# Linear attention with a Mish MLP on one core: the k v product of items 8 and 9 and the copy before the last addition moved, items 4 to 7 worked in pairs, the first sixteen slots in another order

## The chip, the core and the metric

One core of a Trainium2 chip runs the whole program. Its five engines work from queues of their own: TensorE (PE, the matmuls; PEld is its loading of weights), VectorE (DVE), ScalarE (ACT), GpSimd (POOL) and SyncE (SP, which here only issues transfers). An instruction runs when those ahead of it in its queue are done and its semaphores are set. The metric is the time of one execution on the device, in microseconds; the median of several runs is compared.

## The reference

```python
q_s = softmax(q, axis=-1)                 # over the 64 of a head
k_s = softmax(k, axis=2)                  # over the 576 positions
kv  = einsum('bhsd,bhse->bhde', k_s, v)   # 64 x 64 for each head
x   = einsum('bhsd,bhde->bhse', q_s, kv)  # then heads side by side: 4608 x 512
h   = x @ w_in                            # 512 -> 2048
g   = h * tanh(log1p(exp(h)))             # Mish
out = g @ w_out                           # 2048 -> 512
```

q, k and v have 8 batches of 8 heads, 576 positions of 64. All is float32.

## The kernel before

An *item* is a pair of heads of one batch, so there are 32, four to a batch (`HP = 4`); items i and i+1 share what the code calls a pair. An item passes through: loading; q less its maximum, exp, the sum over each head, its reciprocal and the product (`a_qmax`, `a_qsub`, `a_exp`, `a_qsum`, `a_qinv`, `a_qmul`); k less its maximum over positions and exp; the product k^T v with a column of ones beside v, which brings the sum of exp k; its division by that sum into the tile `kvt`, block by block for two items (`a_kvs2`); transposes of q; and x = q kv for both items (`a_xp`, `a_x2`). x is split into a high and a low part, as are the weights, and three products of the parts give one of full precision.

The MLP works on chunks of 512 tokens: nine chunks, and 2048 hidden units in 16 blocks of 128 make 9 × 16 = 144 *slots*. Slot n has an input product H (`h_part`, `ph`, line 543; four parts of three matmuls of 128x512), Mish on ACT (`y`), a high part gh and a low part gl on DVE (`g_hi`, `g_lo`), and, three slots later (`LAG = 3`), an output product O (`out_part`, `po`, line 596; four parts of three matmuls) that adds to the chunk's four PSUM banks a to d. After a chunk's last slot the four banks are evicted (`evac`, `ob`, line 601) and stored. H takes the banks g and h in turn.

The first sixteen slots run while the first batch and the second are prepared and the weights are converted. Their order is written out in the string `FIRST`, one token for a step, for all engines alike: L, LK, LQ, V, R issue loads on SP's queue (k, transposed k, q, v, a weight unit); MQ, SQ, EQ, Q, QZ, QM work on q; MK, KD, KT, EK, B, KS on k; KP, S are k^T v and kvt; T, TC, XT, XP, Z, ZL, ZT, ST the way to x; RA to RS convert weight units (16 of w_in and 16 of w_out) with bit operations on ACT, DVE and POOL; H, Y, G, GL, O the slots (H4f is the first part of slot 1 in bank f). D or A at the end of a step's name means DVE or ACT in place of the usual engine: SD subtracts and QD multiplies q on DVE (SQ, QM: POOL), KD subtracts k's maximum on DVE, RD, RS and RO, RL are the same weight step on DVE or POOL, GA is the high part on ACT (G: DVE). `FILL` adds dummy matmuls ahead of a step so that PE does not sit idle; the SP queue is in the order of the L, R and V tokens. `STAGED` names the buffer into which each weight unit is loaded.

Items 4 to 7, the second batch, keep k as rows of 128 positions: `a_kmax` transposes the maximum with PE (line 303), `a_ksub` subtracts on DVE over 128x640 (line 337), and `a_kvi` multiplies in matmuls of 128 rows by 64 columns, ten for an item (line 447; the profile counts each twice, 40 for a pair). Items from 8 on (`COLS = 8`) come in pairs: the tile of k holds both items, one on partitions 0 to 63 and the other on 64 to 127, and 36 matmuls of 64 rows by 64 columns (line 487; 72 in the profile) serve both.

After `FIRST` the function `group(n)` issues four slots at a time, and with them the steps of later items. At u = 2 of an odd group it calls `a_pair`, which makes x of one pair and k^T v of the next. The group at i = 8 (slots 16 to 19, with slots 13 to 16 as outputs) is an exception:

```python
if u == 2 and front:      # pairs from 8 on
    g_mish(m)
    a_pair(pair)
...
if 0 <= o < NSLOT:
    out_mm(o)
...                       # evictions, g_hi, g_lo, a_kmx
if u == 2 and not front:  # the pair of items 8 and 9
    a_pair(pair)
```

The products of a pair, `pt`, lie in the banks g and h, which the slots use in turn, and `kvt` is read out of them on DVE. The program's end: the outputs of the last three slots are done bank by bank, banks a to c are evicted with ACT and stored, and the last bank's sum of the earlier slots is copied to `base` by ACT (line 711) after that; the rest of its sum is formed in two fresh half banks, added to `base` by DVE (line 717) and stored by ACT's queue and SP's.

Of the kernel before, what the change touches and what calls it, by code (L numbers as in the profile page):

```python
# [15 lines left out]
P = 128  # L16
# [27 lines left out]

FILL = dict(
    KT1=21, KP0=6, T0=2, KT3=4, H0=2)

STAGED = (
    "xb0 xb3 wo4 xb1 wo5 wo6 wo7 xb2 wo8 wo9 wo10 wo11 wo12 wo13 wo14 raw wo6 wo7 xb2 wo8 wo10 wo9 wo11 wo12 wo13 "
    "raw wo14 wo12 wo13 raw wo14 raw")  # L50
# [3 lines left out]
def attn_mish_mlp(ctx: ExitStack, tc: tile.TileContext, q, k, v, k2, v2, wu, qs, kt, out):  # L54
# [4 lines left out]
    HP, D = 4, k.shape[-1]  # L59
# [122 lines left out]
    ap.tile([P, 76], F32, tag="gap0", name="gap0")  # L182
# [8 lines left out]
    v_last = lp.tile([P, 2 * VC], F32, tag="v3", name="v3")  # L191
    v_two = v_last[:, 0:2 * NR * (D + 2)].rearrange("p (h c f) -> p h c f", h=2, f=D + 2)

    def k_load(i):
        if i >= NITEM:
            return
        r = at[i] = at.get(i, {})
        if i >= COLS:
            t = r["k"] = xp.tile([P, NR, 2, D], F32, tag="raw", name=f"k{i}")
            nc.sync.dma_start(t, k2[(i - COLS) // 2])  # L200
            return
        if i == 6:
            t = pools["ke"]
        else:
            pool, tag = (ap, "ke") if i in (4, 7) else (lp, "k3")
            t = pool.tile([P, NC + 1, 2, D], F32, tag=tag, name=f"k{i}")
        r["k"] = t
        nc.sync.dma_start(t, k[i])
# [23 lines left out]
    def v_load(i):  # L232
        if i >= NITEM:
            return
        if i >= COLS:
            nc.sync.dma_start(v_two, v2[(i - COLS) // 2])
            return
        if i < HP:
            at.setdefault(i, {})["v"] = vt[i] if i < HP - 1 else v_last[:, 0:VC]
            nc.sync.dma_start(at[i]["v"], v[i])  # L240
            return
        for j in range(2):
            at.setdefault(i + j, {})["v"] = v_last[:, j * VC:(j + 1) * VC]
        nc.sync.dma_start(v_last.rearrange("p (i f) -> p i f", i=2), v[i:i + 2].rearrange("i p f -> p i f"))

    def a_kmx(i):
# [4 lines left out]
        nc.vector.tensor_reduce(mxd, r["kt"], axis=AX.X, op=ALU.max)  # L251
# [47 lines left out]
    def a_kmax(i, b):  # L299
        r = at[i]  # L300
        pb = bank(b, f"pb{i}")
        fill(f"B{i}", pb)
        nc.tensor.transpose(pb[:, 0:P], r["mxd"].to_broadcast([P, P]), ident)
        r["mb"] = pb[:, 0:P]
# [9 lines left out]
    def a_ktsub(i, eng=nc.vector):  # L314
        r = at[i]
        eng.tensor_scalar(r["kt"], r["kt"], r["mxd"], None, ALU.subtract)
# [15 lines left out]
    def a_ksub(i):  # L332
        if i >= NITEM:
            return
        r = at[i]
        mb = r["mb"].rearrange("p (h d) -> p h d", h=2)
        nc.vector.tensor_tensor(r["k"], r["k"], mb.unsqueeze(1).to_broadcast([P, NC + 1, 2, D]), ALU.subtract)
# [16 lines left out]
    def a_exp(i, which="kq"):  # L354
        if i >= NITEM:
            return
        r = at[i]
        for nm in which:
            if i < COLS:
                e = r[nm]  # L360
            else:
                e = ap.tile([P, NB, 32], F32, tag="qe", name=f"qe{i}")
            nc.scalar.activation(e, r[nm], AF.Exp)  # L363
            r[nm + "e"] = e
# [85 lines left out]
    def a_kvp(e, b):  # L450
        pkv = bank(b, f"pkv{e}")
        fill(f"KP{e}", pkv)
        for i in range(2):
            a_kvi(pkv[:, i * (D + 2):(i + 1) * (D + 2)], e + i)
        at[e]["pkv"] = pkv[:, 0:2 * (D + 2)].rearrange("p (i f) -> p i f", i=2)

    def a_kvs2(e):
        pkv = at[e]["pkv"]
        rs = ap.tile([P, 2], F32, tag="rs0", name=f"rs{e}")
        if e < COLS:  # L460
            nc.vector.tensor_scalar_add(rs, pkv[:, :, D], 1e-9)
            nc.vector.reciprocal(rs, rs)
            nc.vector.tensor_tensor(kvt, pkv[:, :, 0:D], rs.unsqueeze(2).to_broadcast([P, 2, D]), ALU.mult)
            return
# [6 lines left out]
    def a_pair(e):  # L471
# [10 lines left out]
        if f < NITEM:  # L482
            for c in range(NR):
                for j in range(2):
                    for i in range(2):
                        a = slice(i * D, (i + 1) * D)
                        nc.tensor.matmul(pkv[i][j * D:(j + 1) * D], at[f]["k"][a, c, j], v_two[a, j, c],  # L487
                                         start=c == 0, stop=c == NR - 1)
            at[f]["pkv"] = pkv
# [60 lines left out]
    def open_pools():  # L550
# [4 lines left out]
        op = ctx.enter_context(tc.tile_pool(name="op", bufs=1))  # L555
        pools["ke"] = op.tile([P, NC + 1, 2, D], F32, tag="ke", name="ke_odd")
# [22 lines left out]
    def out_mm(n):  # L579
# [4 lines left out]
        for t in range(NC):  # L584
# [26 lines left out]
    def group(n):  # L611
# [4 lines left out]
        front = pair is not None and pair >= COLS  # L616
        for u in range(G):
# [3 lines left out]
            if u == 2 and front:  # L621
                g_mish(m)
                a_pair(pair)
# [13 lines left out]
            if 0 <= o < NSLOT:  # L637
                out_mm(o)
            if m < NSLOT and not (u == 2 and front):
# [36 lines left out]
        a_exp(i + 1, "q")  # L676
# [6 lines left out]
        KD=a_ktsub, KE=lambda i: a_ktsub(i, pool), KT=a_ktt,  # L683
        EK=lambda i: a_exp(i, "k") if i >= HP else a_ktexp(i), EQ=lambda i: a_exp(i, "q"),
# [9 lines left out]
    with tc.manual_schedule(engines={ET.Activation, ET.PE, ET.DVE, ET.Pool, ET.SP}):  # L694
# [9 lines left out]
        end = range(NSLOT - LAG, NSLOT)  # L704
        for t in range(NC - 1):
# [4 lines left out]
        base = sp.tile([P, DM], F32, tag="wc", name="base")  # L710
        nc.scalar.copy(base, po[t])
# [63 lines left out]
```

## Time and profile before

| | |
|---|---|
| median of 3 runs | 862.34 us (861.81 to 862.42) |
| the profiled execution | 863.62 us, span 861.8 us |
| mean granted clock of PE | 0.998 |
| PE, busy | 848.1 us, 98% |
| DVE, ACT, POOL, busy | 434.3, 320.8, 127.4 us |
| PE idle ahead of H, largest releaser | 2.6 us, DVE kvt |

The profiled execution lies 1.3 us above the median. The span runs from the first to the last instruction. A row of the timeline gives the start, the time from the first start to the last end, engine, line, operation and tile, and in square brackets how long the engine sat idle before it and what released it. Consecutive matmuls overlap, so two starts tell more than one duration.

### The profile page before, as it was taken

To read this page: it belongs to the slowest core of one execution; us is meant where nothing else is said; L and a number is where in the kernel's file an instruction comes from. 1 tells how busy PE (TensorE), PEld (TensorE's weight loads), DVE (VectorE), ACT (ScalarE), POOL (GpSimd) and SP (SyncE) were. 2 spreads that over 40 slices of the span, in tenths; PEclk is the share of its full clock that TensorE was granted. 3 is DMA by queue.
4 is the path that set the end of the run, shared out by engine and by line. 5 is a ranking of instruction groups with operands and counts; after the bars stand their busy time and mean duration, and the time that the engine had idled before them with its cause. 6 is when DMAs were issued, how large, how long until landed. Compare 5 with 4: busy or idle time off the path is not lost.

```text
span 861.8 us, 12412 instructions
## 1 busy us (share of the span) xinstructions
PE 848.1 (98%) x4879; PEld 691.6 (80%) x4879; DVE 434.3 (50%) x1113; ACT 320.8 (37%) x496; POOL 127.4 (15%) x111
## 2 busy tenths in 40 slices
PE   8999998999999999999999999999999999999998
PEld 7777777888888888888888888888888888888886
DVE  7989765554655456554645464546543222222221
ACT  5997644424342524333342434243523111111111
POOL 6895310111111111011111001111110000000000
PEclk9999999999999999999999999999999999999999
DMA  9983224212211122212221222122000020001001
GB/s 352 396 313 117 75 100 136 71 41 73 83 46 64 29 86 77 87 29 84 80 74 41 74 80 70 42 60 76 18 15 1 15 74 13 1 0 49 1 1 49
DMA packets 33211, 66.65 MB, mean 77 GB/s; under 512 B 11520, under 2 KB 11776, under 8 KB 33152
## 3 DMA queue, kind: packets, MB, share of 16 engines
q1 hardware_dynamic: 32752, 65.33, 23.0%
q8 instruction: 38, 0.62, 0.3%
q10 hardware_dynamic: 400, 0.52, 0.2%
q14 instruction: 21, 0.17, 0.1%
HBM read 55.35 MB, written 10.49 MB: 76 GB/s over the span
## 4 chain that ended last, share of the span: by engine, by line
PE 88%; DMA 4%; ACT 3%; DVE 3%; issue 1%; SPq 0%; DVEq 0%; ACTq 0%
PE po L596 43%; PE ph L543 42%; PE px L429 2%; DMA q<-in_q_dram 1%; PE pt L487 1%; DMA kt<-in_kt_dram 1%; DMA raw_in<-in_w_dram 1%; ACT wa L132 1%; DVE wa L148 1%; DVE wc_out L154 1%; ACT ph L561 1%; DVE gl L113 0%; DMA raw_out<-in_w_dram 0%; ACT wih L167 0%; DVE mxd L251 0%
## 5 line engine op out<-in xcount | busy, mean ns | idle before, releaser
L543 PE MATMUL ph<-xs,wih 128*128 128x512 f32 x1152 | 357.6, 392 | 5.5 <-DVE kvt L469 2.6
L596 PE MATMUL po<-wo,gh 128*128 128x512 f32 x1146 | 355.1, 391 | 0.0
L543 PEld LDWEIGHTS ph<-xs,wih 128*128 128x128 f32 x1152 | 215.6, 188 | 53.8 <-issue 3.5
L596 PEld LDWEIGHTS po<-wo,gh 128*128 128x128 f32 x1146 | 214.3, 188 | 45.4 <-issue 0.8
L565 ACT ACTIVATE y<-ph 128x512 f32<-128x512 f32 x128 | 76.5, 597 | 422.6 <-PE ph L543 355.8
L543 PE MATMUL ph<-xs,wil 128*128 128x512 f32 x576 | 225.1, 391 | 0.0
L596 PE MATMUL po<-wo,gl 128*128 128x512 f32 x573 | 223.1, 389 | 0.0
L570 DVE CAST gh<-y 128x512 fp32r<-128x512 f32 x128 | 55.3, 432 | 271.1 <-ACT y L565 271.1
L543 PEld LDWEIGHTS ph<-xs,wil 128*128 128x128 f32 x576 | 108.4, 188 | 22.7
L596 PEld LDWEIGHTS po<-wo,gl 128*128 128x128 f32 x573 | 107.6, 188 | 22.6
L113 DVE TENSOR_TENSOR gl<-y,gh 128x512 fp32r<-128x512 f32 x128 | 89.4, 698 | 11.9
L386 POOL TENSOR_TENSOR qe<-qe,qs 128x576 f32<-128x576 f32 x24 | 27.8, 1160 | 304.0 <-DVE qs L382 304.0
L113 POOL TENSOR_TENSOR q<-q,qm 128x576 f32<-128x576 f32 (+1 forms) x31 | 36.6, 1182 | 191.3 <-DVE qm L270 174.3
L565 ACT ACT_TABLE_LOAD x23 | 29.5, 1283 | 49.0 <-PE ph L543 48.9
L523 DVE TENSOR_TENSOR xs<-px,xs 128x512 fp32r<-128x512 f32 x32 | 20.7, 686 | 49.6 <-ACT xs L520 49.6
L372 DVE TENSOR_REDUCE qs<-qe 128x18 f32<-128x576 f32 x24 | 18.0, 752 | 25.8 <-ACT qe L363 25.8
L352 ACT ACT_TABLE_LOAD x23 | 29.5, 1283 | 2.4 <-DVE k L113 2.0
L279 DVE TENSOR_REDUCE qm<-q 128x18 f32<-128x576 f32 (+1 forms) x32 | 24.3, 762 | 4.9 <-DMA q<-in_q_dram 4.8
L251 DVE TENSOR_REDUCE mxd<-kt 128x1 f32<-128x576 f32 x32 | 23.8, 745 | 2.4 <-DMA kt<-in_kt_dram 2.4
L601 DVE COPY ob<-po 128x512 f32<-128x512 f32 x16 | 11.1, 691 | 26.9 <-PE po L596 26.8
L113 POOL TENSOR_TENSOR wo<-wc_out,wo 128x512 fp32r<-128x512 f32 x15 | 19.4, 1295 | 23.3 <-ACT wo L167 23.2
L363 ACT ACT_TABLE_LOAD x16 | 20.5, 1283 | 4.3 <-DMA q<-in_q_dram 4.0
(112 smaller groups left out, 563.3 us busy)
## 6 DMA issues: line engine op xcount, KB each, us to landing
kt<-in_kt_dram SPq DMA_DIRECT2D x32, 288.0 KB, 2.8
raw_in<-in_w_dram SPq DMA_DIRECT2D x16, 512.0 KB, 8.6
raw_out<-in_w_dram SPq DMA_DIRECT2D x16, 512.0 KB, 6.3
out_dram<-ob SPq DMA_DIRECT2D x32, 256.0 KB, 2.2
v<-in_v_dram SPq DMA_DIRECT2D x12, 594.0 KB, 5.3
q<-in_qs_dram SPq DMA_DIRECT2D x24, 288.0 KB, 2.8
k<-in_k_dram SPq DMA_DIRECT2D x12, 576.0 KB, 4.1
q<-in_q_dram SPq DMA_DIRECT2D x8, 320.0 KB, 6.1
```

The lines of the kernel that those rows point to most:

```text
L113: eng.tensor_tensor(out, a, b, ALU.subtract)
L251: nc.vector.tensor_reduce(mxd, r["kt"], axis=AX.X, op=ALU.max)
L279: nc.vector.tensor_reduce(qm, qt, axis=AX.X, op=ALU.max)
L352: nc.scalar.activation(k2, k2, AF.Exp)
L363: nc.scalar.activation(e, r[nm], AF.Exp)
L372: nc.vector.tensor_reduce(z, q2, axis=AX.X, op=ALU.add)
L386: eng.tensor_tensor(q2, q2, z.unsqueeze(2).to_broadcast(list(q2.shape)), ALU.mult)
L523: nc.vector.tensor_tensor(xs[i][:, 1], src, xs[i][:, 0].bitcast(F32), ALU.subtract)
L543: nc.tensor.matmul(gs[n], wi[a][:, t, fs], x[:, z], start=t == 0 and i == 0, stop=t == HP - 1 and i == 2)
L565: nc.scalar.activation(y, gs[n], AF.Mish)
L570: copy(hi, gs[n])
L596: nc.tensor.matmul(dst, g[a][:, t * P:(t + 1) * P], wo[f][:, z, e], start=first and i == 0, stop=last and i == 2)
```

## The change

1. *The group at i = 8.* `a_pair`, which here makes k^T v of items 8 and 9, is called in the same place as for the later ones, after `g_mish`, and slot 15's output is cut in two: banks a and b ahead of the pair's products, c and d behind them.
2. *The end.* The copy to `base` is issued before the last three slots' outputs and the three evictions.
3. *Items 4 to 7* are loaded, subtracted, exponentiated and multiplied in pairs, as items from 8 on: `in_k_dram` is gone, the layouts of `in_k2_dram` and of `in_v2_dram` begin at item 4, one k load of 576 KB stands in place of two of 320, `a_kmax` puts both maxima in a bank with two matmuls of 64 columns, and `a_kv2` is the 36 matmuls as a function.
4. *The first sixteen slots.* `FIRST`, `FILL` and `STAGED` are new. Three of the first four subtractions of k's maximum run on ACT (token KA, with the maximum negated by its reduction, `negate=i < HP`), one on DVE. Three products of q run on DVE (QD), none did; no subtraction of q does (SD), one did. Of the high parts of the first 16 slots 7 run on ACT, 6 did.

```diff
 FIRST = (
-    "LQ1 LQ0 LK1 LK0 LK2 LQ2 V1 MQ1 LQ3 V0 MQ0 SQ1 LK3 R0 V2 MK1 SQ0 EQ1 V3 MK0 R1 LQ4 KD1 R2 KD0 KT1ab R3 EQ0 MQ2 "
+    "LQ0 LK0 LK1 LQ1 LQ2 LQ3 V2 MQ0 V0 LK2 MK0 SQ0 V1 LK3 KA0 R0 MK1 EQ0 R1 KT0ab MQ1 R2 V3 KD1 LK4 MQ2 SQ1 KT1cd "
...
 FILL = dict(
-    KT1=21, KP0=6, T0=2, KT3=4, H0=2)
+    KT0=14, KT1=4, KP0=12, XT0=3, H1=4)
...
-        if i >= COLS:
-            t = r["k"] = xp.tile([P, NR, 2, D], F32, tag="raw", name=f"k{i}")
-            nc.sync.dma_start(t, k2[(i - COLS) // 2])
-            return
...
+        t = r["k"] = lp.tile([P, NR, 2, D], F32, tag="kk", name=f"k{i}")
+        nc.sync.dma_start(t, k2[(i - HP) // 2])
...
-        tag = f"xa{i}" if i < HP else "k3" if i > COLS and i % 2 else "kt"
+        tag = f"xa{i}" if i < HP else "kt" if i % 2 else "kt2"
...
+        if i >= HP:
+            nc.sync.dma_start(v_two, v2[(i - HP) // 2])
+            return
...
-        nc.vector.tensor_reduce(mxd, r["kt"], axis=AX.X, op=ALU.max)
+        nc.vector.tensor_reduce(mxd, r["kt"], axis=AX.X, op=ALU.max, negate=i < HP)
...
-    def a_kmax(i, b):
-        r = at[i]
-        pb = bank(b, f"pb{i}")
-        fill(f"B{i}", pb)
-        nc.tensor.transpose(pb[:, 0:P], r["mxd"].to_broadcast([P, P]), ident)
+    def a_kmax(e, b):
+        pb = bank(b, f"pb{e}")
+        fill(f"B{e}", pb)
+        for j in range(2):
+            nc.tensor.matmul(pb[j * D:(j + 1) * D, 0:P], at[e + j]["mxd"].to_broadcast([P, D]), ident, start=True, stop=True)
...
+    def a_ktsub_act(i):
+        r = at[i]
+        nc.scalar.activation(r["kt"], r["kt"], AF.Identity, bias=r["mxd"])
...
+    def a_kexp(e):
+        nc.scalar.activation(at[e]["k"], at[e]["k"], AF.Exp)
...
+    def a_kv2(e, pkv):
+        for c in range(NR):
+            for j in range(2):
+                for i in range(2):
+                    a = slice(i * D, (i + 1) * D)
+                    nc.tensor.matmul(pkv[i][j * D:(j + 1) * D], at[e]["k"][a, c, j], v_two[a, j, c],
+                                     start=c == 0, stop=c == NR - 1)
...
-        if e < COLS:
+        if e < HP:
             nc.vector.tensor_scalar_add(rs, pkv[:, :, D], 1e-9)
...
-    def out_mm(n):
+    def out_mm(n, parts=range(NC)):
...
-        for t in range(NC):
+        for t in parts:
             out_part(n, t)
...
-            if u == 2 and front:
+            split = u == 2 and pair is not None
+            if split:
                 g_mish(m)
+                if pair < COLS:
+                    out_mm(o, (0, 1))
                 a_pair(pair)
...
-                out_mm(o)
-            if m < NSLOT and not (u == 2 and front):
+                out_mm(o, (2, 3) if split and pair < COLS else range(NC))
+            if m < NSLOT and not split:
                 g_mish(m)
...
-                    if not front:
-                        a_pair(pair)
...
         end = range(NSLOT - LAG, NSLOT)
+        base = sp.tile([P, DM], F32, tag="wc", name="base")
+        nc.scalar.copy(base, po[NC - 1])
         for t in range(NC - 1):
...
-        base = sp.tile([P, DM], F32, tag="wc", name="base")
-        nc.scalar.copy(base, po[t])
```

Three places show how the instructions are moved. First DVE in the group at i = 8, before. `rs` and `kvt` are the division of the products `pt`, `ob` an eviction, `gh` and `gl` of slot 18, `mxd` and `mb` k's maximum for later items:

```order
L601 COPY ob0_0_1576<-po0_0_563 128x512
L601 COPY ob0_2_1582<-po0_2_565 128x512
L570 CAST gh18_1588<-y18_1574 128x512
L113 TENSOR_TENSOR gl18_1590<-y18_1574,gh18_1588 128x512
L251 TENSOR_REDUCE mxd11_1592<-kt11_1488 128x1
L260 STREAM_TRANSPOSE mb10_1529<-mxd11_1592 32x32 x4
L261 COPY mb10_1529<-mb10_1529 32x128
L466 TENSOR_SCALAR rs8_1639<-pt6_0_1601 128x1
L466 TENSOR_SCALAR rs8_1639<-pt6_1_1602 128x1
L467 RECIPROCAL rs8_1639<-rs8_1639 128x2
L469 TENSOR_TENSOR kvt_83<-pt6_0_1601,rs8_1639 128x64
L469 TENSOR_TENSOR kvt_83<-pt6_1_1602,rs8_1639 128x64
```

And the same engine and place after:

```order
L464 TENSOR_SCALAR rs8_1635<-pt6_0_1597 128x1
L464 TENSOR_SCALAR rs8_1635<-pt6_1_1598 128x1
L465 RECIPROCAL rs8_1635<-rs8_1635 128x2
L467 TENSOR_TENSOR kvt_83<-pt6_0_1597,rs8_1635 128x64
L467 TENSOR_TENSOR kvt_83<-pt6_1_1598,rs8_1635 128x64
L591 COPY ob0_0_1647<-po0_0_576 128x512
L591 COPY ob0_2_1653<-po0_2_578 128x512
L560 CAST gh18_1659<-y18_1589 128x512
L113 TENSOR_TENSOR gl18_1661<-y18_1589,gh18_1659 128x512
L237 TENSOR_REDUCE mxd11_1663<-kt11_1515 128x1
L246 STREAM_TRANSPOSE mb10_1556<-mxd11_1663 32x32 x4
L247 COPY mb10_1556<-mb10_1556 32x128
```

The division has moved ahead of the evictions, of slot 18's parts and of the maximum.

Second, PE around the k v product of items 4 and 5 in the first slots, before (`ph6` is slot 6, `xs3` the fourth part of x, `wih` and `wil` the weights' parts):

```order
L543 MATMUL ph6_780<-xs2_483,wih_86 128x512 x2
L543 MATMUL ph6_780<-xs2_483,wil_87 128x512
L543 MATMUL ph7_786<-xs2_483,wih_86 128x512 x2
L543 MATMUL ph7_786<-xs2_483,wil_87 128x512
L447 MATMUL pkv4_827<-v3_94,k4_179 64x66 x10
L447 MATMUL pkv4_827<-v3_94,k5_394 64x66 x10
L543 MATMUL ph6_780<-xs3_477,wih_86 128x512 x2
```

And after:

```order
L535 MATMUL ph5_670<-xs3_473,wih_86 128x512 x2
L535 MATMUL ph5_670<-xs3_473,wil_87 128x512
L535 MATMUL ph6_740<-xs1_382,wih_86 128x512 x2
L535 MATMUL ph6_740<-xs1_382,wil_87 128x512
L451 MATMUL pkv4_765<-v3_94,k4_184 64x66
L451 MATMUL pkv4_1_766<-v3_94,k4_184 64x66
```

The product stood ahead of the last parts of slots 6 and 7, and now stands after the second part of slot 6 (its matmuls alternate between two banks, of which the first two are shown). Slot 3's output was ahead of it, and no longer is.

Third, SP's queue of loads at the last weight units, before (`raw_in` and `raw_out` are weight units of w_in and w_out, `q6` and `q7` the queries of items 6 and 7):

```order
L126 DMA raw_in15_1017<-in_w_dram 128x1024
L126 DMA raw_out12_1039<-in_w_dram 128x1024
L126 DMA raw_out13_1045<-in_w_dram 128x1024
L126 DMA raw_out14_1063<-in_w_dram 128x1024
L230 DMA q6_1070<-in_q_dram 128x640
L230 DMA q7_1089<-in_q_dram 128x640
```

And after:

```order
L126 DMA raw_in15_1002<-in_w_dram 128x1024
L126 DMA raw_out12_1009<-in_w_dram 128x1024
L221 DMA q6_1038<-in_q_dram 128x640
L126 DMA raw_out13_1073<-in_w_dram 128x1024
L126 DMA raw_out14_1090<-in_w_dram 128x1024
L221 DMA q7_1136<-in_q_dram 128x640
```

The load of q 6 is two weight units earlier in the queue, that of q 7 is not.

More of the change, by code (lines that the diff above doesn't have):

```diff
@@ L181, in attn_mish_mlp @@
     xs = {}
-    ap.tile([P, 76], F32, tag="gap0", name="gap0")
+    ap.tile([P, 12], F32, tag="gap0", name="gap0")
     early = ap.tile([P, 1], F32, tag="early", name="early")
@@ L190, in attn_mish_mlp @@
     vt = [pp.tile([P, VC], F32, tag=f"v{j}", name=f"v{j}") for j in range(HP - 1)]
-    v_last = lp.tile([P, 2 * VC], F32, tag="v3", name="v3")
-    v_two = v_last[:, 0:2 * NR * (D + 2)].rearrange("p (h c f) -> p h c f", h=2, f=D + 2)
+    v_last = lp.tile([P, 2 * NR * (D + 2)], F32, tag="v3", name="v3")
+    v_two = v_last.rearrange("p (h c f) -> p h c f", h=2, f=D + 2)
     def k_load(i):
@@ L234, in v_load @@
             return
-        if i >= COLS:
-            nc.sync.dma_start(v_two, v2[(i - COLS) // 2])
+        if i >= HP:
+            nc.sync.dma_start(v_two, v2[(i - HP) // 2])
             return
[L238 to L244, printed above, removed]
+        at.setdefault(i, {})["v"] = vt[i] if i < HP - 1 else v_last[:, 0:VC]
+        nc.sync.dma_start(at[i]["v"], v[i])
     def a_kmx(i):
@@ L312, in attn_mish_mlp, with a_ktsub @@
         ks.append(t)
-    def a_ktsub(i, eng=nc.vector):
+    def a_ktsub(i):
         r = at[i]
-        eng.tensor_scalar(r["kt"], r["kt"], r["mxd"], None, ALU.subtract)
+        nc.vector.tensor_scalar(r["kt"], r["kt"], r["mxd"], None, ALU.add)
+    def a_ktsub_act(i):
+        r = at[i]
+        nc.scalar.activation(r["kt"], r["kt"], AF.Identity, bias=r["mxd"])
     def a_ktt(i, b):
@@ L330, in a_ktexp, with a_ksub @@
         nc.scalar.activation(t[0:ST, NC].rearrange("p h d -> p (h d)"), pk2[0:ST, 0:P], AF.Exp)
[L332 to L337, printed above, removed]
+    def a_ksub(e):
+        k2, mb = at[e]["k"], at[e]["mb"].rearrange("p (h d) -> p h d", h=2)
+        sub(nc.vector, k2, k2, mb.unsqueeze(1).to_broadcast(list(k2.shape)))
     parts = slice(0, NC + 1), slice(NC + 1, NR)
@@ L352, in a_exp2, with a_exp @@
         nc.scalar.activation(k2, k2, AF.Exp)
-    def a_exp(i, which="kq"):
+    def a_exp(i):
         if i >= NITEM:
@@ L357, in a_exp @@
         r = at[i]
[L358 to L364, printed above, removed]
+        e = r["qe"] = r["q"] if i < COLS else ap.tile([P, NB, 32], F32, tag="qe", name=f"qe{i}")
+        nc.scalar.activation(e, r["q"], AF.Exp)
+    def a_kexp(e):
+        nc.scalar.activation(at[e]["k"], at[e]["k"], AF.Exp)
     def a_qsum(i):
@@ L450, in a_kvp @@
     def a_kvp(e, b):
-        pkv = bank(b, f"pkv{e}")
+        pkv = bank(b[0], f"pkv{e}")
         fill(f"KP{e}", pkv)
-        for i in range(2):
-            a_kvi(pkv[:, i * (D + 2):(i + 1) * (D + 2)], e + i)
-        at[e]["pkv"] = pkv[:, 0:2 * (D + 2)].rearrange("p (i f) -> p i f", i=2)
+        if e < HP:
+            for i in range(2):
+                a_kvi(pkv[:, i * (D + 2):(i + 1) * (D + 2)], e + i)
+            at[e]["pkv"] = pkv[:, 0:2 * (D + 2)].rearrange("p (i f) -> p i f", i=2)
+        else:
+            a_kv2(e, [pkv[:, 0:D + 2], bank(b[1], f"pkv{e}_1")[:, 0:D + 2]])
+    def a_kv2(e, pkv):
+        for c in range(NR):
+            for j in range(2):
+                for i in range(2):
+                    a = slice(i * D, (i + 1) * D)
+                    nc.tensor.matmul(pkv[i][j * D:(j + 1) * D], at[e]["k"][a, c, j], v_two[a, j, c],
+                                     start=c == 0, stop=c == NR - 1)
+        at[e]["pkv"] = pkv
     def a_kvs2(e):
@@ L482, in a_pair @@
         if f < NITEM:
[L483 to L489, printed above, removed]
+            a_kv2(f, pkv)
         if px:
@@ L615, in group @@
         pair = i - 1 if i % 2 and COLS < i < NITEM else COLS - 2 if i == COLS else None
-        front = pair is not None and pair >= COLS
         for u in range(G):
@@ L682, in attn_mish_mlp @@
         MK=a_kmx, MQ=a_qmax, SQ=a_qsub, SD=lambda i: a_qsub(i, dve), B=a_kmax, KS=a_ksub,
-        KD=a_ktsub, KE=lambda i: a_ktsub(i, pool), KT=a_ktt,
-        EK=lambda i: a_exp(i, "k") if i >= HP else a_ktexp(i), EQ=lambda i: a_exp(i, "q"),
+        KD=a_ktsub, KA=a_ktsub_act, KT=a_ktt,
+        EK=lambda i: a_kexp(i) if i >= HP else a_ktexp(i), EQ=a_exp,
         KP=a_kvp,
@@ L756 @@
         "in_q_dram": rows(q, 8, True),
-        "in_k_dram": rows(k, 8, True),
-        "in_v_dram": ones(rows(v, 8, False).transpose(0, 1, 3, 2, 4)).reshape(8, 128, -1),
+        "in_v_dram": ones(rows(v, HP, False).transpose(0, 1, 3, 2, 4)).reshape(HP, 128, -1),
         "in_k2_dram": two(k),
```

24 lines of the change are left out of this document (8 added, 16 removed), and 40 rows, old and new, of the table FIRST.

## The prediction

> **What bounds the kernel now.** I read the page's totals first, then busy time by stretch, then the chain of waits and the timelines at the places that these pointed to.
>
> ```profile
> PE 848.1 (98%) x4879; PEld 691.6 (80%) x4879; DVE 434.3 (50%) x1113; ACT 320.8 (37%) x496; POOL 127.4 (15%) x111
> ...
> 10.00:30.00 20.00, 18.63 (x194) 14.06 (x193) 18.32 (x45) 17.26 (x41) 16.78 (x13) 1.00 1.03 409
> 36.00:48.00 12.00, 11.56 (x51) 8.99 (x50) 12.00 (x21) 10.27 (x20) 9.90 (x8) 1.00 1.02 390
> 48.00:60.00 12.00, 10.64 (x75) 8.22 (x75) 10.13 (x21) 10.69 (x18) 11.39 (x9) 1.00 0.88 299
> 60.00:72.00 12.00, 12.00 (x65) 9.69 (x62) 10.22 (x20) 9.84 (x16) 6.74 (x7) 1.00 0.34 109
> 72.00:84.00 12.00, 11.33 (x53) 8.28 (x51) 11.47 (x22) 8.95 (x18) 8.55 (x7) 1.00 0.47 141
> 84.00:96.00 12.00, 10.54 (x51) 8.32 (x52) 8.00 (x13) 7.83 (x16) 3.40 (x3) 1.00 0.31 115
> 96.00:120.00 24.00, 24.00 (x156) 17.71 (x155) 15.01 (x36) 16.03 (x29) 6.76 (x6) 1.00 0.32 103
> 140.00:144.00 4.00, 4.00 (x13) 3.09 (x12) 0.00 (x0) 0.00 (x0) 0.00 (x0) 0.61 0.88 282
> 144.00:862.00 718.00, 713.67 (x4018) 586.18 (x4016) 321.02 (x876) 223.23 (x320) 52.19 (x45) 1.00 0.16 48
> ```
>
> Columns after the window and its length: busy time of PE, PEld, DVE, ACT, POOL, then the granted clock, the DMA share and GB/s. PE is the bound throughout. From 144 us its busy time falls 718.00 − 713.67 = 4.3 us short of the window, which is the end of the span after its last matmul, so the steady part has nothing to give. Three places remain: the first slots, where PE sits idle 0.44 + 1.36 + 0.67 + 1.46 = 3.9 us between 36 and 96 us; the four microseconds from 140, at a clock of 0.61; and the end. The change touches all three.
>
> The chain of waits around the second place, and the timelines of PE and DVE:
>
> ```profile
> 133.21 2.05 PE po L596 x9
> ...
> 139.34 0.36 DVE kvt L469 x2
> 139.71 4.46 PE ph L543 x12
> 144.17 1.98 PE po L596 x8
> ```
> ```profile
> 135.86 1.28 PE L487 MATMUL pt<-v,k 64*64 64x66 f32 x72
> 139.71 0.70 PE L543 MATMUL ph<-xs,wih 128*128 128x512 f32 x2 [2.57 <-DVE kvt L469]
> ...
> 142.69 1.05 PE L543 MATMUL ph<-xs,wih 128*128 128x512 f32 x2
> ```
> ```profile
> 135.29 0.69 DVE L601 COPY ob<-po 128x512 f32<-128x512 f32 x1 [0.67 <-PE po L596]
> ...
> 137.74 0.86 DVE L260 STREAM_TRANSPOSE mb<-mxd 32x32 f32<-32x32 f32 x4
> ...
> 138.88 0.23 DVE L466 TENSOR_SCALAR rs<-pt 128x1 f32<-128x1 f32 x2
> ...
> 139.34 0.35 DVE L469 TENSOR_TENSOR kvt<-pt,rs 128x64 f32<-128x64 f32 x2
> ```
>
> PE has slot 15's output behind it and runs the short products (72 in the profile's count) of items 8 and 9, done by 137. They lie in the two banks that the slots take in turn, so slot 19 may start only when DVE has made kvt of them, and DVE first does an eviction, gh, gl, the maximum of k of item 11 and its transposes. PE idles 2.57 us, and most of slot 19 then runs at half rate: twelve matmuls in 4.46 us.
>
> **The repair at item 8.** In the order of after, the five kvt operations stand ahead of the evictions and gh 18, and slot 15's output is cut: six matmuls before item 8's products, six after. A slot's twelve matmuls take 2.72 us, as this row of the same chain shows:
>
> ```profile
> 130.49 2.72 PE ph L543 x12
> ```
>
> so six cover 1.36 us. The kvt operations last from 138.88 to 139.70, 0.8 us; with a handover of 0.1, 0.9 of the 1.36. The stall goes. What is now queued behind kvt on DVE comes later: products from 134.57 to 135.62, kvt to 136.5, then two evictions of 0.69 to 137.9, gh and gl to 139.0. Slot 16's output, next in these banks, starts at 139.7, slot 18's two slots on: both are covered, the first by 1.8 us. The products start 1.36 us earlier. Their bank needs slot 18's Mish, 0.6 us on ACT behind 133.21: done near 134.0, 0.5 us to spare. And exp of items 8 and 9 ended at 130.98 on ACT:
>
> ```profile
> 129.72 1.26 ACT L352 ACTIVATE k<-k 128x640 f32<-128x640 f32 x2
> ```
>
> against a need at 134.57, 3.6 us of cover. Without the stall slot 16's output starts at 130.49 + 2.72 + 2.72 + 1.05 + 2.72 = 139.70, where it started at 144.17: **−4.5 us**, of which 2.8 are the pause and 1.7 the half rate. The 1.05 is the same 72 products in a steady pair: first start 161.6, last 162.6:
>
> ```profile
> L487 PE MATMUL pt<-v,k x72: 215/218/221, 161.6 to 162.6; 64*64 64x66 f32 x72
> ```
>
> [...]
>
> **The repair at the end.**
>
> ```profile
> 857.02 0.58 ACT L711 COPY base<-po 128x512 f32<-128x512 f32 x1 [0.87 <-ACT ob L601]
> ...
> 857.39 0.28 PE L596 MATMUL po_last<-wo,gl 128*128 128x256 f32 x1
> 857.64 0.76 DVE L717 TENSOR_TENSOR ob<-po_last,base 128x256 f32<-128x256 f32 x2 [9.02 <-ACT base L711]
> 858.09 1.38 ACTq L609 DMA_DIRECT2D out_dram<-ob  x2
> ```
>
> The two last additions on DVE (857.64 to 858.40) wait for ACT's copy of base. With the copy some microseconds earlier, the first runs at 856.5, when its half of the bank is done, and the second when PE ends, 857.67. The second then starts where now the first does, and its DMA issue no longer queues behind the first's on ACT: between 0.3 (one addition) and 0.7 us (one issue, 1.38/2). I take **−0.4**; nothing at worst, since ACT idled ahead of that copy.
>
> **Items 4 to 7 by pairs.**
>
> ```profile
> 19.38 1.39 PE L447 MATMUL pkv<-v,k 128*64 128x66 f32 x40
> 20.70 0.66 PE L406 MATMUL pq<-ident,q 128*128 128x128 f32 x4
> ```
>
> Forty products take 20.70 − 19.38 = 1.32 us; the 72 of the other form 1.05. Two pairs: −0.54. Four transposes of the maximum become two pairs of 64-column matmuls: equal within 0.1. I take **−0.6** as the two together. [...] On the other engines the pairs cost nothing that PE sees as long as these are ahead of it: DVE's two subtractions of 1152 columns take at most as long as the four of 640 now; ACT's exp likewise (row below); kvt of 4 and 6 gains two small operations each, some 0.3 us on the path to nothing nearer than X products two slots on.
>
> **The new order of the first slots.** It is bounded from before's rows. Ahead of slot 0 PE waits for kvt and fills the time:
>
> ```profile
> 14.07 0.71 PE L297 MATMUL pq<-kvt 128*128 128x128 f32 x4 [0.69 <-DVE kvt L463]
> ...
> 22.78 0.71 PE L543 MATMUL ph<-xs,wih 128*128 128x512 f32 x2
> ```
>
> After has two groups of transposes standing ahead of that wait, so its first slot can start up to 1.6 us earlier (0.69 of wait, the rest fills that are dropped there). Against that SP's queue now loads kt 4 and the k of items 4 and 5 in one 576 KB tile ahead of the fourth weight unit: 256 + 288 KB more, at the 409 GB/s of the first window 1.3 us later weights, and POOL's conversions follow. I set the two against each other: **+0.3** at slot 0's output. From there on the waits of before, with the row that starts each:
>
> ```profile
> 53.95 0.75 DVE L251 TENSOR_REDUCE mxd<-kt 128x1 f32<-128x576 f32 x1 [1.30 <-DMA kt<-in_kt_dram]
> ...
> 87.91 1.61 DVE L279 TENSOR_REDUCE qm<-q 128x10 f32<-128x640 f32 x2 [1.84 <-DMA q<-in_q_dram]
> ```
> ```profile
> 55.36 0.73 PE L543 MATMUL ph<-xs,wih 128*128 128x512 f32 x2 [1.36 <-DVE gl L113]
> ...
> 84.84 0.73 PE L543 MATMUL ph<-xs,wih 128*128 128x512 f32 x2 [0.91 <-ACT qT L421]
> ```
>
> DVE's queue stands still until a late kt lands, and the gl behind it holds PE 1.36 us; then it stands still for q of items 6 and 7, whose loads came behind four weight units. After issues q 6 two units earlier and reserves the kt loads ahead. PE's 3.9 us, with 0.2 or so at each of seven restarts, come to 5.3. I take four fifths as gone, **−4.3**, and give back **+0.6** for the last slots of the stretch, where weight units 31 now share ACT and DVE with the conversions of slot 14. Work that changes engine here (three q products from POOL to DVE, three subtractions of k and one hi cast from DVE to ACT, one q subtraction and one weight rest from DVE to POOL) moves by single instructions of 0.5 to 1.3 us; PE's path carries them only where their engine is late, which the give-back holds. With the pairs: 0.3 − 4.3 + 0.6 − 0.6 = **−4.0**, with ends of −6.9 (5.3 of waits and the 1.6 all gained) and +2.9 (the weights' 1.3, the 0.6, and 1.0 at the spot below, nothing gained).
>
> The tightest spot is the kv product of items 4 and 5:
>
> ```profile
> 46.52 0.64 ACT L132 ACTIVATE wa<-raw_out 128x512 f32<-128x512 f32 x1
> 47.09 0.61 ACT L167 CAST wih<-wc_in 128x512 fp32r<-128x512 f32 x1
> ...
> 55.91 1.35 ACT L363 ACTIVATE k<-k 128x640 f32<-128x640 f32 x2
> ...
> 59.01 1.39 PE L447 MATMUL pkv<-v,k 128*64 128x66 f32 x40
> ```
>
> Now exp ends 1.75 us before it is used. After has 26 parts of slots and 3 outputs ahead of the product, not 30 and 4: 4 × 0.68 + 2.72 = 5.4 us of PE's work less. ACT has eight conversions less, at 47.09 − 46.52 = 0.57 each, and three subtractions of k more, which I price at 0.6 from exp's 0.67 for 640 columns: 2.7 us less. If both queues ran as late as now PE would wait 5.4 − 2.7 − 1.75 = 1.0 us there. I count on ACT being less late, as it waits for fewer loads.
>
> **Sum.** −4.5 − 0.4 − 4.0 = −8.9 us. The profiled execution took 863.62, 1.28 above the median of 862.34: 854.7 for it, **853.4** for the median.
>
> **The rivals.** (a) The new order gains nothing: waits move to the later weights and PE ends its first slots where it did. Then the repairs remain: 862.3 − 4.5 − 0.4 = 857.4. For it: PE's idle time there is only 3.9 us in 60, with DMA at 0.88 to 1.03 in the windows before 60 us, so what is put ahead delays something else. (b) The pause at item 8 moves: slot 18's Mish or the eviction behind kvt comes late, and PE waits there as long, 862.3 − 0.4 − 4.0 = 857.9. For it: 0.5 us of cover at the Mish is little; against it, such a miss would cost tenths, not the 4.5 us. (c) The half rate has its own cause and stays: 853.4 + 1.7 = 855.1. (d) Slower: exp of items 4 and 5 holds PE at their kv product. ACT would be later than now, by weights 1.3 us later and three subtractions on it; the wait is 1.0 us plus ACT's further lateness, and past 2.5 us it costs 1.7 us of half rate too. The change stops paying when wait and half rate eat 5.5 us (all but the order's own gain), at ACT 2.8 us later than now; with 5 us later the time is 862.3 − 5.5 + 6.0 + 1.7 = 864.5. Against it: ACT was busy 10.69 of the 12 us there, so it can catch up, and the pair's exp is one instruction.
>
> **Chances.** Forecast 0.61; (a) 0.20; (b) 0.05; (c) 0.05; (d) 0.09. Of (d) 0.06 ends above 864.1 and 0.03 within 0.2% of the median, which is about what a measurement of this kernel tells from no change; of (a) 0.02 falls there. So faster 0.89, same 0.05, slower 0.06. The range takes in (a), (b), (c): from 850.2, which is 862.3 − 6.9 − 4.5 − 0.7, to 859.2, which is 862.3 less the pause of 2.8 and the end's 0.3. The forecast's own range is 851 to 856.
>
> **What would show it.** Right: after slot 15's first half the products of item 8 run, slot 19 follows without a pause and the clock stays at 1.00 there; the last additions sit on both sides of PE's end; slot 16's output starts near 144.2 − 4.5 − 4.0 = 135.7. Wrong: a wait of PE for kvt near item 8; PE waiting over 2 us at the kv product of items 4 and 5, with exp as the releaser; PE waits for weight conversions between 25 and 40 us.

## The result, and the profile after

The changed kernel takes 857.75 us (857.49 to 858.41, 4 runs) against 862.35 (861.81 to 862.42, 4 runs): 4.6 us less. The ratio on record is 0.9937, 95% interval 0.9924 to 0.9950, which would be 5.4 us; it is not the quotient of the two medians (0.9947), but its interval holds that too. Forecast were 853.4, with a range of 850.2 to 859.2. The sign was right and the time lies in that range, which had been stretched to take in the rivals; it lies outside the forecast's own range of 851 to 856, and half to three fifths of the expected 8.9 us came. The profiled execution of after took 857.9 us, span 856.1, close to its median; that of before had lain 1.3 us above its own, which turns out to matter.

First the page's totals and the busy time by stretch, with the columns as before (PE, PEld, DVE, ACT, POOL, granted clock, DMA share, GB/s):

```profile
PE 846.2 (99%) x4951; PEld 690.4 (81%) x4951; DVE 433.3 (51%) x1111; ACT 322.8 (38%) x498; POOL 127.9 (15%) x111
...
10.00:30.00 20.00, 17.86 (x201) 14.15 (x200) 18.88 (x44) 18.26 (x42) 16.19 (x13) 1.00 1.03 407
36.00:48.00 12.00, 12.00 (x54) 8.97 (x53) 11.65 (x19) 11.30 (x22) 11.84 (x10) 1.00 1.01 385
48.00:60.00 12.00, 12.00 (x120) 9.84 (x119) 10.64 (x27) 11.94 (x19) 11.51 (x9) 1.00 0.95 342
60.00:72.00 12.00, 12.00 (x56) 9.43 (x55) 11.74 (x19) 9.47 (x17) 9.18 (x8) 1.00 0.26 90
72.00:84.00 12.00, 11.86 (x56) 9.23 (x55) 11.07 (x21) 10.06 (x19) 10.39 (x8) 1.00 0.62 202
84.00:96.00 12.00, 11.00 (x55) 8.50 (x54) 8.70 (x17) 9.66 (x16) 3.77 (x3) 1.00 0.12 32
140.00:144.00 4.00, 4.00 (x20) 3.30 (x19) 0.98 (x2) 0.03 (x1) 0.00 (x0) 1.00 0.92 329
144.00:857.00 713.00, 708.05 (x3992) 580.95 (x3990) 319.23 (x873) 222.84 (x319) 52.23 (x45) 1.00 0.16 49
```

Between 36 and 96 us PE now idles 0.14 + 1.00 = 1.1 us, where it was 3.9. From 10 to 30 us it idles more, 2.1 us, where it was 1.4 (18.63 busy). The four microseconds from 140 are full, at clock 1.00. The chain of waits of after around item 8 (start, length, what, instructions):

```profile
128.68 2.72 PE ph L535 x12
131.40 1.36 PE po L586 x6
132.76 1.21 PE pt L451 x72
133.97 1.57 PE po L586 x6
135.54 2.72 PE ph L535 x12
138.26 2.72 PE po L586 x12
```

Slot 15's first half, the products, the second half and slot 19 follow without a pause; DVE's division is off the chain. PE's rows of after that show a wait or the pair:

```profile
26.50 1.16 PE L283 MATMUL ph<-kvt 128*128 128x128 f32 x8 [1.77 <-DVE wc_in L154]
...
53.25 1.28 PE L451 MATMUL pkv<-v,k 64*64 64x66 f32 x72
54.47 0.73 PE L535 MATMUL ph<-xs,wih 128*128 128x512 f32 x2
...
85.50 0.73 PE L535 MATMUL ph<-xs,wih 128*128 128x512 f32 x2 [1.00 <-ACT qT L406]
```

The first is new, the last is the wait that before had at 84.84. Read as positions (first starts of matmuls), slot 0's input starts at 21.93 (before 22.78), its output at 36.40 (34.87), slot 18's input at 128.51 (130.33) and slot 16's output at 138.10 (143.97). So the place at item 8 gave 5.87 − 1.82 = 4.05 us between these two executions, and the first slots 1.8. Of the prediction's signs, slot 16's output comes 2.4 us later than the 135.7 named, and one of the signs of being wrong is there: at 26.50 PE waits 1.77 us for a weight conversion.

### The profile page after: what moved, and what is told of

It reads as the page before. It is cut to its first block, busy times and chain, and to the rows that moved or that the text cites. A ratio compares the mean times of both kernels' runs of the same rounds, so it can differ in the third digit from the quotient of the medians.

```text
span 856.1 us, 12563 instructions
## 1 busy us (share of the span) xinstructions
PE 846.2 (99%) x4951; PEld 690.4 (81%) x4951; DVE 433.3 (51%) x1111; ACT 322.8 (38%) x498; POOL 127.9 (15%) x111
## 4 chain that ended last, share of the span: by engine, by line
PE 90%; DMA 4%; DVE 3%; ACT 1%; issue 1%; SPq 1%; POOL 0%; DVEq 0%
PE po L586 44%; PE ph L535 42%; PE px L414 2%; DMA raw_out<-in_w_dram 2%; DMA v<-in_v_dram 2%; PE pt L451 2%; DMA k<-in_k_dram 1%; DVE wa L148 1%; DVE wc_out L154 1%; DVE k L113 0%; DVE wc_in L154 0%; DVE gl L113 0%; PE po_last L586 0%; PE pt L414 0%; SPq L209 0%
## 5 line engine op out<-in xcount | busy, mean ns | idle before, releaser
L246 DVE STREAM_TRANSPOSE mb<-mxd 32x32 f32<-32x32 f32 x96 | 19.4, 202 | 1.8
L113 POOL TENSOR_TENSOR wil<-wc_in,wih 128x512 fp32r<-128x512 f32 x15 | 19.4, 1305 | 5.6 <-ACT wih L167 5.2
```

Of the source, the lines that this page charges most:

```text
L113: eng.tensor_tensor(out, a, b, ALU.subtract)
L246: nc.vector.transpose(mb[o:o + 32, h], mxd[h].to_broadcast([32, 32]))
```

## The experiments

All times of one group come from the same chip, with runs of the kernel before between them. Two explanations of the shortfall were to be told apart first. Theory A: item 8 is worth what the profiled execution of before shows. Theory B: the half rate behind its pause comes in some executions only. Eleven runs were made, one of them the changed kernel again. Where a gain stands behind a ratio, it is worked out from that ratio; the difference of the medians beside it can be up to 0.6 us larger, and each interval reaches about 1 us to both sides.

### The repairs alone and left out

Item 8 alone, in the kernel before:

```diff
-            if u == 2 and front:
+            split = u == 2 and pair is not None
+            if split:
                 g_mish(m)
+                if pair < COLS:
+                    out_mm(o, (0, 1))
                 a_pair(pair)
...
-                out_mm(o)
+                out_mm(o, (2, 3) if split and pair < COLS else range(NC))
...
```

> The kernel before with the repair at item 8 alone. In the profiled executions this place went from 13.68 us (slot 18's start to slot 16's output) to 9.58, so theory A (pause and half rate stand in every execution of before) expects 4.1 us less than before, a ratio of 0.9952. Theory B (the half rate behind the pause comes in some executions only, the profiled one among them, which is why the profiled spans differ by 5.7 us and the medians by 4.6) expects 2.5 to 3.0 us less, 0.9965 to 0.9971. Both expect no wait of PE for kvt in the profile.

Measured 859.91 against 862.96 us, 0.9970 (0.9957 to 0.9983): 2.6 us less (3.1 by the medians). Theory A's 0.9952 lies outside the interval, theory B's band inside.

The end alone:

```diff
+        base = sp.tile([P, DM], F32, tag="wc", name="base")
+        nc.scalar.copy(base, po[NC - 1])
         for t in range(NC - 1):
...
-        base = sp.tile([P, DM], F32, tag="wc", name="base")
-        nc.scalar.copy(base, po[t])
```

> The kernel before with the copy to base moved ahead alone. The prediction's step says 0.4 us less (0.3 to 0.7). The traces of before and after say 0.1 to 0.2: from PE's last matmul to the end of the second addition 0.73 us before and 0.52 after, to the end of the span 4.13 and 4.05. The pause at item 8 stays; its half rate is to be seen here a second time (theory A) or is missing or shorter (theory B).

Measured 0.9997 (0.9986 to 1.0008), too coarse for tenths. In its trace the span ends 3.65 us after PE's last matmul, where before has 4.16: 0.5 us, inside the prediction's 0.3 to 0.7 and more than was expected here. It also shows the pause at item 8 a second time; the timeline of PE:

```profile
136.55 1.28 PE L487 MATMUL pt<-v,k 64*64 64x66 f32 x72
140.39 0.70 PE L543 MATMUL ph<-xs,wih 128*128 128x512 f32 x2 [2.56 <-DVE kvt L469]
...
141.62 0.40 PE L543 MATMUL ph<-xs,wil 128*128 128x512 f32 x1
141.86 0.62 PE L543 MATMUL ph<-xs,wih 128*128 128x512 f32 x2
```
```profile
140.40:144.00 3.60, 3.60 (x16) 2.97 (x17) 0.00 (x0) 0.57 (x1) 0.00 (x0) 1.00 1.00 336
```

The same pause, 2.56 us, and behind it full rate: two matmuls in 0.62 us, not 1.05, clock 1.00. From slot 18 to slot 16's output it is 12.21 us here, 13.64 before, 9.6 where there is no pause.

Both repairs (the two edits together):

> Both repairs, with the first slots and items 4 to 7 as before. Theory A expects 4.1 + 0.15, so 4.2 us less than before and the new first slots with the pairs to be worth only the rest of the 4.6, about 0.4. Theory B expects 2.7 to 3.1 us less, with 1.5 to 1.9 left for the first slots, as the traces show (slot 18 starts 1.81 us earlier).

Measured 859.44 us, 0.9966 (0.9953 to 0.9979): 2.9 us less, theory B's number (3.5 by the medians), and the trace's tail is 3.64 us again. What is left for the first slots and pairs is fixed only roughly by the times: 2.5 us by the ratios (0.9937 for the whole change), 1.1 to 2.0 by the medians.

The changed kernel without the repair at item 8 (the first diff reversed):

> The changed kernel with the pair of items 8 and 9 back in its old place and slot 15's output whole; first slots, pairs and end as changed. Theory A expects 4.1 us more than the changed kernel (some 861.9 us), theory B 2.5 to 3.0 more (860.3 to 860.8). Its profile shows the pause for kvt again, and whether the clock falls behind it.

Measured 861.35 us, 0.9987 (0.9977 to 0.9998) of before, 3.6 us more than the changed kernel's 857.75 by the medians and 4.3 by the ratios: this time does not tell the theories apart. Its timeline and its stretches show the pause with half rate:

```profile
137.74 0.70 PE L535 MATMUL ph<-xs,wih 128*128 128x512 f32 x2 [2.56 <-DVE kvt L467]
...
139.93 1.06 PE L535 MATMUL ph<-xs,wih 128*128 128x512 f32 x2
```
```profile
139.00:142.00 3.00, 3.00 (x9) 2.32 (x8) 0.00 (x0) 0.00 (x0) 0.00 (x0) 0.55 0.64 252
```

The mean granted clock of every execution speaks for theory B. Of 24 of before in this group, 14 had 0.997 or 0.998 and took 863.5 us on average, 10 had 0.999 and took 861.8; the seven of the kernel with item 8 repaired all had 0.999 or 1.0. The mean does not say where in an execution the clock was lower, and one of the first four executions of the changed kernel, without the pause, shows 0.998 too (858.41 us); but in the three traces with the pause mean and half rate go together (0.998 and 0.997 with it, 1.0 without). So, by the mean clocks, the half rate follows the pause in some six of ten executions (14 of 24) and costs 1.4 us (13.64 − 12.21) to 1.7 (863.5 − 861.8) there. By positions in the traces, repairing item 8 is worth 2.6 us without it and 4.1 with it, 3.5 on average. The times of the repair alone say less: its mean of 859.9 lies 1.9 us below the executions of before with the higher clock and 3.6 below the others. Part of that gap stands behind item 8: from slot 16's output to PE's last matmul the traces of the two repaired kernels take 714.1 and 714.2 us, where that of before takes 713.7. Why is open.

### The pause shortened, and the early slots

The kernel before with the maximum of k 11 moved behind the division:

```diff
-            if i == COLS and u < 3:
+            if i == COLS and u < 2:
                 a_kmx(i + 1 + u)
...
+            elif i == COLS and u == 2:
+                pass
...
                     if not front:
                         a_pair(pair)
+                        a_kmx(i + 1 + u)
+                        kt_load(i + 3 + u)
```

> The kernel before, with only the maximum of k of item 11 and its transposes (1.84 us on DVE) moved behind the division at item 8. The pause should fall from 2.57 to 0.7 us. If the half rate comes from the length of the pause, it is absent in the profile and the time falls by 1.85 us and by the half rate's share in the executions of before, together 2 to 3 us (0.9965 to 0.9977). If it comes from the short products ahead of the pause, half rate is still seen in some executions and the time falls by 1.85 us only.

Measured 860.12 us, 0.9972 (0.9960 to 0.9984): 2.4 us less. From slot 18 to slot 16's output 10.52 us, 0.9 more than without a pause (PE idles 4.00 − 3.18 = 0.82 us from 136 to 140 us); no half rate in the profile (clock 1.00 from 136 to 145 us), and all eight runs at 0.999 or 1.0, where six of the twelve of before in this group had 0.997 or 0.998. So here the half rate goes with the pause of 2.57 us and not with the short products ahead of it. The time does not decide that, since its interval holds both expectations; the clock does.

The changed kernel again, as neighbour of the next ones:

> The changed kernel unaltered, so that the three variants beside it have their neighbour on the same chip. By the traces so far its parts are worth 1.9 us (first slots with the pairs), 2.6 to 4.1 (item 8, without and with the half rate), 0.1 (end) and -0.2 (steady part): 4.4 to 5.9 us less than before, a ratio of 0.9932 to 0.9949.

857.42 us, 0.9938 (0.9925 to 0.9952): 5.3 us less than before here, 5.6 by the medians.

On it, weight unit 2's two DVE steps (`RB2 RC2`) ahead of the maxima `MK4 MQ4`, and x's high parts (`Z2 Z3`) ahead of `RA4 RM4`:

```diff
-    "RL3 H1 RA3a MK4 RH1 XT2bc MQ4 LK6 RA4d XP2fg RO1 RB2 ZT3 ZT2 RM4 ST3 RB3 ST2 Z2 SQ4 RC2 LK5 Z3 H4e ..."
+    "RL3 H1 RB2 RC2 RA3a MK4 RH1 XT2bc MQ4 LK6 XP2fg RO1 Z2 ZT3 ZT2 Z3 RA4d RM4 ST3 RB3 ST2 SQ4 LK5 H4e ..."
```

> The changed kernel with two moves in the first slots: on DVE the two steps of weight unit 2 (whose scratch holds the bank of slot 1) ahead of the maxima of k 4 and q 4, and on ACT the high parts of x 2 and x 3 ahead of the steps of weight unit 4. Theory 'the early loss is queue order': PE's pause of 1.8 to 2.2 us ahead of slot 1 falls under 0.5 us, slot 0's output starts 1.5 to 2 us earlier, the time falls by 1 to 1.9 us (0.9978 to 0.9988 of the changed kernel). Theory 'the early loss is late weight data and a full DVE': PE waits at the next weight unit instead, slot 0's output starts within 0.5 us of where it did, and the time stays.

858.11 us, against its neighbour's 857.42: not faster. The wait ahead of slot 1 is gone, and two stand in its place:

```profile
26.48 0.50 PE L535 MATMUL ph<-xs,wil 128*128 128x512 f32 x1 [1.01 <-POOL wil L113]
31.35 0.70 PE L535 MATMUL ph<-xs,wih 128*128 128x512 f32 x2 [0.96 <-DVE wc_in L154]
```

Slot 0's output starts at 36.27 (neighbour 35.75). So the place of these steps in their queues did not hold slot 0's output.

The changed kernel with q 5's copy ahead of weight unit 30's step:

```diff
-... T5fh RM30 H47 RD27 LQ7 TC5 RA28f ...
+... T5fh TC5 H47 RD27 LQ7 RM30 RA28f ...
```

> The changed kernel with the copy of q 5's transposes on ACT moved ahead of the step of weight unit 30, whose load is late there. Theory: PE's wait near 84 us (1.0 to 1.1 us, for that copy, behind ACT's wait for the load) goes, and the time falls by 0.8 to 1.2 us (0.9986 to 0.9991 of the changed kernel). Rival: the wait moves to the bank or weight that unit 30 serves, and less than 0.4 us is left.

856.06 us (855.95 to 857.21) against 857.42: 1.4 us less, 0.9923 (0.9911 to 0.9935) of before. Four of its five executions lie below the fastest of the changed kernel's five, so this version beats both kernels. The rows of ACT, first of after, then of this variant:

```profile
84.21 0.66 ACT L136 ACTIVATE raw_out<-raw_out 128x512 uint32<-128x512 uint32 x1 [0.71 <-DMA raw_out<-in_w_dram]
84.77 0.57 ACT L405 COPY qT<-pq 128x512 f32<-128x512 f32 x1
```
```profile
82.80 0.59 ACT L405 COPY qT<-pq 128x512 f32<-128x512 f32 x1 [0.15 <-PE pq L391]
83.28 0.22 ACT L406 COPY qT<-pqt 128x64 f32<-128x64 f32 x1
83.39 0.66 ACT L136 ACTIVATE raw_out<-raw_out 128x512 uint32<-128x512 uint32 x1
```

In after ACT stood still for a late weight unit with the copy behind it that PE needed. With the copy first, PE's wait is gone and the weight is not missed.

On that variant, the loads of the second batch put later (the move of `TC5` is not shown again):

```diff
-... R2 V3 KD1 LK4 MQ2 SQ1 KT1cd LQ4 EK0 L4 Q0 EK1 R3 SQ2 MQ3 R4 EQ1 ... R8 ...
+... R2 V3 KD1 MQ2 SQ1 KT1cd EK0 Q0 EK1 R3 SQ2 MQ3 R4 LK4 LQ4 EQ1 ... R8 L4 ...
```

and `MK4` behind `RB4`, `MQ4 SQ4` behind `RB5`.

> On top of the copy of q 5 moved ahead: the loads of kt 4, q 4 and of k 4 and 5 go behind weight units 4 and 8 in SP's queue, and the maxima of k 4 and q 4 on DVE, with the subtraction on POOL, behind weight unit 4's steps. The prediction's step (weights 1.3 us late cost what the earlier start gains) says that the pause ahead of slot 1 shrinks from 1.6 us to under 0.5 and slot 0's output starts about 1.3 us earlier, at 34.5 to 35: 1 to 1.4 us less than the variant with q 5 alone. Rival, after the run with unit 2 early: DVE and POOL set the pace until slot 3, whatever lands; slot 0's output starts within 0.4 us of 36, and the time stays.

857.25 us, against 856.06 of the variant with q 5 alone in the group before; ratios to before 0.9932 and 0.9923, so no gain. PE's rows:

```profile
24.39 1.16 PE L283 MATMUL ph<-kvt 128*128 128x128 f32 x8 [0.27 <-DVE wc_in L154]
31.17 0.70 PE L535 MATMUL ph<-xs,wih 128*128 128x512 f32 x2 [1.47 <-DVE wc_in L154]
37.15 0.50 PE L586 MATMUL po<-wo,gh 128*128 128x512 f32 x1 [0.70 <-POOL wo L113]
```

The first wait shrank as the step said, from 1.58 in the variant it is built on (1.77 in after) to 0.27, but the next units' conversions hold PE at 31 and 37 us, and slot 0's output starts at 36.06. The rival holds.

The loads late and unit 2 early, both on the variant with q 5 ahead:

> The same and also unit 2's two DVE steps and the high parts of x 2 and x 3 ahead, as tried alone before, where PE then waited 1.0 us for POOL's low part of unit 1 and 1.0 us for unit 3 on DVE. If late data was behind these, both waits fall with the loads moved and slot 0's output starts by 34.5; if the engines' work is, they stay and the time is that of the variant without this move, within 0.5 us.

856.78 us, within 0.5 of the last; slot 0's output at 35.71. The wait for POOL's low part is gone, so late data was behind that one; the 1.47 us for unit 3's conversion on DVE stand. Neither expectation came whole, but slot 0's output did not come to 34.5 as late data would have had it.

K's maximum back on DVE:

```diff
-... LK3 KA0 R0 ... MK3 KA2 R11 ... R12 KA3 R13 ...
+... LK3 KD0 R0 ... MK3 KD2 R11 ... R12 KD3 R13 ...
```

> The changed kernel with the three subtractions of k's maximum back from ACT to DVE. If DVE is what holds the start (busy 18.9 of the 20 us from 10 to 30), three operations of some 0.5 us more on it delay slot 0 and its output by 1 to 1.5 us, and the time rises by as much against the changed kernel. If ACT holds it (18.3 of 20), the time falls by up to 0.6.

857.75 us; 0.9939 against the changed kernel's 0.9938 and 0.9937: no difference that can be measured. Slot 0's input starts at 22.33, against 21.93 and 21.50 in the two traces of the changed kernel, its output at 36.56, against 36.40 and 35.75. The expected 1 to 1.5 us is a miss; between these traces the subtractions on ACT bring 0.4 to 0.8 us at slot 0, and little of it lasts.

## Why the prediction was right or wrong

**What bounds the kernel** held: the steady part hardly changed (713.5 to 713.7 us from slot 16's output to PE's last matmul in the traces of before and of the end alone, 713.9 to 714.0 in those of the changed kernel with and without the repair at item 8), and all of the gain lies in the three places named.

**Item 8, −4.5: mechanism right, size wrong.** The pause is gone, nothing moved into its place and the clock there is 1.00; rivals (b) and (c) fell. Three things made the term smaller. The 1.7 us of half rate were read from one execution, and some six in ten have it, as the clocks say. The profiled execution of before was one of those at the lower clock, 1.3 us above the median, and the prediction took that as an offset of the run when it was, at least in part, the effect itself. Last, the products with slot 15's halves on both sides take 1.21 + 1.57 us, not 1.05 + 1.36. Of these 0.37 us, 0.16 lie in the price itself: 1.05 is about the time from the first product's start to the last one's. To the start of the next matmul it is 1.17 us in the steady pair too (161.62 to 162.78), and 1.21 at item 8. The way in and out costs the rest: 0.09 us more from the last 128x512 matmul to the products, and 0.12 more in the first part behind them (0.80 us to the next part, not 0.68).

What decides whether half rate follows the pause is not shown: a pause of 2.56 us was followed by full rate in the trace of the end alone (clock 1.00 from 140.4 to 144 us), pauses of 2.57 and 2.56 by half rate in those of before (0.61 from 140 to 144) and of the changed kernel without the repair at item 8 (0.55 from 139 to 142).

**The end, −0.4: right alone, lost in the change.** Alone it brought 0.5 us in the trace, in two kernels. In the changed kernel, as in its variant without item 8, the tail is 4.08 and 4.07 us, 0.1 shorter than before. DVE's second addition ends 0.5 us after PE there too; most of the difference appears in the closing exchange of semaphores, where POOL's next event comes 0.34 us after its last drain, and 0.05 in the kernels built on before. Why is open.

**Items 4 to 7, −0.6: about −0.2.** The 72 products last from 53.25 to 54.47, 1.22 us against 1.32, not 1.05. The sum compared unlike measures: 1.32 ran to the start of the next matmul and 1.05 did not. The way in and out is no reason here: the 40 products of before stood between 128x512 matmuls too, and it was the same (0.32 us from the matmul ahead to the first product in both kernels, 0.81 and 0.80 us to the next part behind). The pairs were not run alone.

**The first slots.** The step "+0.3 at slot 0's output" failed by 0.8 us. Its two parts came: slot 0 starts 0.8 us earlier in the first two traces (1.4 on average of those named next), and PE waits 1.6 to 2.2 us for weights. But its output starts 1.1 us later than in the kernels with the old order (36.1 on average of three traces against 35.0 of five). The step put that on weights landing late. The runs with loads moved show it otherwise: taking away the late data moves the wait to the next unit, and slot 0's output stays near 36. DVE is busy 18.88 and ACT 18.26 of the 20 us from 10 to 30, largely with the conversions ahead of it. That the bound is their work rather than an order not tried is the likeliest reading, not proven: with three operations more on DVE and three fewer on ACT, slot 0's output moved by only 0.2 to 0.8 us.

From there on the step "four fifths of 5.3 us" was half right, and 1.3 us were lost in it. The waits behind late kt loads went, idle time fell from 3.9 (3.0 to 4.0 in other traces of the old order) to 1.1 us (1.1 to 1.3), and slot 18 came 3.0 us nearer to slot 0's output, for −4.3 − 0.6 + 0.6 forecast. The 5.3 itself was too large: no row gives 0.2 us at a restart, and behind the wait at 84.84 the first part takes 0.1 more than the next (0.80 us, then 0.69). The wait of 1 us near 85 us was expected to go and stayed. The prediction had read it wrongly: DVE's wait for q of items 6 and 7 ends at 87.91 and began at 86.07, after PE had gone on at 84.84. A row of before that it does not show has the releaser:

```profile
83.54 0.67 ACT L136 ACTIVATE raw_out<-raw_out 128x512 uint32<-128x512 uint32 x1 [1.19 <-DMA raw_out<-in_w_dram]
```

ACT stood still for a late weight unit there, as it does in after for unit 30, with the copies for PE behind it, so the loads of q 6 and q 7 were not what PE waited for. The 0.6 us given back at the end of the stretch was not needed. The tightest spot was dangerous as said, but the wait of 1.0 us did not come: in after exp of items 4 and 5 ends at 52.71, 0.5 us ahead of its use at 53.25, PE does not wait, and rival (d) fell.

```profile
51.56 1.15 ACT L349 ACTIVATE k<-k 128x1152 f32<-128x1152 f32 x1
```

**Sum by the runs:** −3.5 for item 8, −1.9 for the first slots with the pairs (slot 18 at 128.2 on average of three traces, 130.1 of five), −0.1 at the end, +0.3 in the steady part: −5.2, where two groups measured 4.6 and 5.6 us by the medians and 5.3 to 5.4 by the ratios. The numbers of rivals (b), 857.9, and (a), 857.4, are the nearest to the 857.75 and 857.42 measured, by luck: nothing waits at item 8, and the new order gained half, while the repair brought less than it was given.

## What to carry to other kernels

A profiled execution that lies above its median need not be just shifted: before pricing a stall from it, look at the granted clock of the other executions, since here the same pause, 2.56 to 2.57 us, was followed by half rate in two traces and by full rate in a third. Price a matmul group from its first start to the start of what follows, and with its way in and out: ours cost 0.37 us more at item 8 than the time between its first and last starts had said. When a wait is taken away early in a pipeline whose other engines are over nine tenths busy (here DVE 18.88 and ACT 18.26 of 20 us), look first for the next instruction that these owe, and where one of them waits for a load, for short work queued behind it that the bound engine needs.

## What the runs showed of the hardware

The same pause of PE, 2.56 to 2.57 us, was followed by half rate in two traces (clock 0.55 to 0.61 for some 3 us) and by full rate in a third; 14 of 24 executions of the kernel before show a lower mean clock and 1.7 us more on average. Where PE waits also changes between executions with the same first slots: in one trace of the old order DVE waited 1.30 us for a kt load, and PE 1.36 us at 55 us behind it; in the four others, of kernels that differ from it only later on, PE has no wait near 55 us, and waited 0.5 to 1.0 us at 67 to 69 us for a conversion on DVE instead.
